# A convolution and locality-routed experts on one core: 512-row blocks by seven products, with whole sequences routed at once

## The chip, the cores and the metric

One core of one Trainium2 chip runs the kernel. The metric is device time in microseconds (us), the median of several runs. TensorE is called PE in the profile, VectorE DVE, ScalarE ACT, GpSimd POOL, and SP is the queue that issues most transfers.

## The reference

The input x has 8 sequences of 3584 tokens with 192 channels (28672 tokens in all). A causal convolution of 7 taps, whose taps are a softmax per head (8 heads of 24 channels), gives y. Then each token is routed to one of 8 experts and goes through that expert's two layers, everything in float32:

```
logits = y @ w_gate                       # [.., 8]
local  = sigmoid(y @ w_local)
e[s]   = argmax(logits[s]) if s == 0 or local[s] < 0.5 else e[s-1]
out[s] = softmax(logits[s])[e] * (relu(y[s] @ w1[e]) @ w2[e])   # w1 192x1024, w2 1024x192
```

An expert can be carried over from the token before, so routing is a scan along the sequence.

## The kernel before

**Groups.** Tokens are cut into 16 groups of 1792 (half a sequence), 14 per partition. `load_x` brings a group with a halo of 6 tokens; `conv` makes y with one ACT tap and six DVE taps for each head (L377, L387). `logits` transposes y on DVE (L570), does 96 matmul records (L580) and copies the result back; `route` finds expert, probability and slot with some 90 small DVE operations; `put` scatters 128 rows of y at a time into the DRAM array `slots`, sorted by expert (L775, POOL). Groups 0 and 1 take a faster way, `wide` and `wide_route`, before the first block.

**Blocks.** `slots` is worked off in blocks of rows of one expert. A table written by DVE (`table`) gives each block its first unit of 128 rows and its expert; SP reads an entry into a register and loads the rows (`load_rows`, L911) and the expert's weights (`load_w`, L904, 1.5 MB). A block number stands for a row count fixed when the kernel is built; only which rows and which expert is decided on the chip. There are 55 blocks of 128 rows ("singles": 35 in front, while few tokens are routed, and 20 at the end for what is left over; two more wait behind a test that reads the table) and 87 of 256 rows ("pairs"). A pair that the table marks full can be fixed ahead because so many tokens routed guarantee so many full pairs (`_sure`).

**One block.** `turn` transposes rows on PE (L359) and ACT copies them to xT (L949). D = 192 is three pieces of 64 rows, and w1 lies so that the two halves of PE's rows work on the two halves of F at once. `hidden` does h = relu(x w1) (L963 on PE, L968 on ACT), `output` does h w2 (L980), scales one half on ACT (L988), scales and adds the other on DVE (L992), and POOL sends the rows to their tokens (L996). The heart of `hidden` before is

```
for two in range(2):
    hps = [hps_p.tile([P, 2, BT], F32, name="hps") for half in range(2)]
    for d in range(KD):                    # 3 pieces of D
        for j in range(2):
            for half, rows in halves():    # L963: 24 matmuls a block, 48 records
                nc.tensor.matmul(hps[half][:, j, w], lhsT=wb[rows, f0:f0 + P], rhs=xT[rows, d, w], ...)
```

Other lines that are named below: L223 a POOL copy of y for the front's transposes, L298 a one-column POOL add of constants, L453 a transpose in `wide_route`, L550 the one-hot matrices of the first two blocks' gather, L682 the one-hot of the experts in `route`.

**The order.** Everything is written out by hand. Block i issues hidden(i), the transposes of block i+1, output(i). Between them `step(t)` issues DVE work of `conv` and `route` until the times that their `yield`s state add up to t; scatters hang behind chosen PE or ACT instructions. `ensure` loads rows up to three blocks ahead and, where a group that a block needs isn't routed or scattered yet, forces the work at once. Weights are loaded three blocks ahead into four buffers.

Of the kernel before, what the change touches and what calls it, by code (L numbers as in the profile page):

```python
# [33 lines left out]
NX = NT + HALO  # L34
# [4 lines left out]
KT = BT // P  # L39
# [4 lines left out]
EARLY = 3  # L44
SPARE = 2

# [5 lines left out]


ONE = [_sure(min(g + 1, EARLY) * PT, UT) for g in range(NPART)]
TWO = [_sure((g + 1) * PT - ONE[-1] * UT, BT) if g >= EARLY else 0 for g in range(NPART)]


HALF = 0.5
FULL = {0: ONE[0], HALF: _sure(PT + PT // 2, UT), **{g: ONE[g] for g in range(1, NPART)}}
REST = NU - ONE[-1] - 2 * TWO[-1]  # L60
# [21 lines left out]
def kernel(  # L82
# [13 lines left out]
    xs = ctx.enter_context(tc.tile_pool(name="xs", bufs=2))  # L96
    ys = ctx.enter_context(tc.tile_pool(name="ys", bufs=4))
# [3 lines left out]
    xp = ctx.enter_context(tc.tile_pool(name="xp", bufs=6))  # L101
    tp = ctx.enter_context(tc.tile_pool(name="tp", bufs=1))
    hp = ctx.enter_context(tc.tile_pool(name="hp", bufs=1))
    op = ctx.enter_context(tc.tile_pool(name="op", bufs=2))
    xps_p = ctx.enter_context(tc.tile_pool(name="xps_p", bufs=1, space=PSUM))
    hps_p = ctx.enter_context(tc.tile_pool(name="hps_p", bufs=4, space=PSUM))
    yps_p = ctx.enter_context(tc.tile_pool(name="yps_p", bufs=2, space=PSUM))
# [6 lines left out]
    def load_x(g):  # L114
        x_sb = xs.tile([P, NX, D], F32, name="x_sb")
        src = x[g // PER]
        win = bass.AP(tensor=src.tensor, offset=src.offset + g % PER * PT * D,
                      ap=[[NT * D, P], [1, NX * D]])
        nc.sync.dma_start(out=x_sb.rearrange("p t d -> p (t d)"), in_=win)
        return x_sb  # L120

    def load_b(g):

        x_sb = xs.tile([P, NX, D], F32, name="x_sb")
        xv = x_sb.rearrange("p t d -> p (t d)")[:, :NB * D].rearrange("p (b d) -> p b d", d=D)
        for b in (slice(0, NH), slice(NH, NB)):
            nc.sync.dma_start(out=xv[:, b, :], in_=xb[g, :, b, :])
        return xv
# [9 lines left out]
    with tc.tile_pool(name="scr", bufs=1) as scr:  # L138
# [4 lines left out]
        x_in = {0: load_b(0)}  # L143
        wg = cst.tile([P, 3 + DQ, Q], F32, name="wg")
        nc.sync.dma_start(out=wg, in_=wgl)
        x_in[1] = load_b(1)
# [43 lines left out]
    def z_tile():  # L190
        return yt.tile([P, 3 * NH * TB + NB * DR], F32, name="z")
# [3 lines left out]
    def wide(g, xv, y_sb, both):  # L195
# [58 lines left out]
        yr = zy[:TB, 3 * NH * TB:].rearrange("p (b d) -> p b d", d=DR)  # L254
# [17 lines left out]
        lt = sm.tile([P, NB, E + 1], F32, name="lt")[:TB]  # L272
# [9 lines left out]
    pi = cst.tile([P, 2], I32, name="pi")  # L282
    nc.gpsimd.iota(pi, pattern=[[0, 2]], base=0, channel_multiplier=1)
    ti0 = cst.tile([P, NT], I32, name="ti0")
    nc.gpsimd.iota(ti0, pattern=[[1, NT]], base=0, channel_multiplier=NT)
# [10 lines left out]
    pf = cst.tile([P, 2], F32, name="pf")  # L296
    nc.gpsimd.tensor_copy(pf, pi)
    nc.gpsimd.tensor_tensor(pf[:, 1:], pf[:, 1:], pf[:, :1], op=Alu.add)  # L298
# [32 lines left out]
    cum = cst.tile([P, 1 + E * NT], F32, name="cum")  # L331
# [5 lines left out]
    nc.sync.dma_start(out=slots[DUMMY * UT:(DUMMY + 1) * UT], in_=pad)  # L337
# [8 lines left out]
    tab = [cst.tile([P, 3], F32, name=f"tab{k}") for k in range(3)]  # L346
    ends = [cst.tile([P, 1 + E], F32, name=f"ends{k}") for k in range(3)]
    for k in range(3):
        nc.gpsimd.memset(tab[k], 0.0)
        nc.gpsimd.memset(ends[k], 0.0)  # L350
# [12 lines left out]
    def row_tile():  # L363
        return ys.tile([P, NB, DG], F32, name="y_sb")

    def conv(g, x_sb):
        y_sb = row_tile()[:, :NT, :]
        got[g] = y_sb

        def cols(h):  # L370
            return y_sb[:, :, Y0 + h * GS:Y0 + (h + 1) * GS]

        def chans(h, k):
            return x_sb[:, k:k + NT, h * GS:(h + 1) * GS]

        def first(h):
            nc.scalar.activation(cols(h), chans(h, 0), Act.Copy, scale=c[:, h, 0:1])  # L377

        first(0)
        yield 0  # L380
        for h in range(H):
            if h + 1 < H:
                first(h + 1)
            if h == H // 2 and 2 < g < NPART - 1:
                x_in[g + 1] = load_x(g + 1)
            for k in range(1, KC):
                nc.vector.scalar_tensor_tensor(cols(h), chans(h, k), c[:, h, k:k + 1],  # L387
                                               cols(h), Alu.mult, Alu.add)
                yield 0.6
# [3 lines left out]
    def wide_route(g, y_sb, lt):  # L393
# [16 lines left out]
        ex = sm.tile([P, NB, E], F32, name="ex")[:TB]  # L410
# [3 lines left out]
        eq = sm.tile([P, NB, E], F32, name="eq")[:TB]  # L414
# [13 lines left out]
        def norm():  # L428
            nc.vector.tensor_reduce(rs, ex, axis=AX.X, op=Alu.add)
            nc.vector.tensor_scalar(rs, rs, 1e-9, None, Alu.add)  # L430
            nc.vector.reciprocal(rs, rs)
# [42 lines left out]
        upto = sm.tile([P, E, 1 + NB], F32, name="upto")  # L474
# [90 lines left out]
    def logits(g, y_sb):  # L565

        z = z_tile()[:, :NT * D].rearrange("p (t d) -> p t d", d=D)
        for t in range(0, NT, TQ):
            u = min(t + TQ, NT)
            nc.vector.transpose(z[:, t:u, :], y_sb[:, t:u, Y0:Y0 + D])  # L570
            yield 0.2 * (u - t)
        yield "hop"


        lps = [hps_p.tile([P, TQ * Q], F32, name="hps") for half in range(2)]
# [658 lines left out]
```

## Time and profile before

| | us |
|---|---|
| median of 3 runs (1315.73 to 1316.56) | 1316.22 |
| the profiled execution | 1326.81 |
| its span, first to last instruction | 1325.1 |
| PE busy | 1304.4 |
| DVE busy | 778.3 |
| ACT busy | 625.2 |
| POOL busy | 480.4 |
| PE records L963 (hidden), union | 637.2 |
| PE records L980 (output), union | 641.0 |

DMA read 277.29 MB and wrote 45.77 MB, 244 GB/s over the span. The mean granted clock of TensorE was 0.998. In the profile's groups a line is: place in the code, engine, operation, output <- inputs, shapes, count | busy time, mean of one in ns | idle time before them and what ended it. In the order of time a line is: start, length, engine, place, operation, and how many were merged; [idle before <- what ended it].

### The profile page before, as it was taken

The numbers are of one execution on the slowest core, as the hardware profiler recorded it, in microseconds if no ns is written. First come the engines' busy times: TensorE is split into PE (matmuls) and PEld (weight loads), VectorE is DVE, ScalarE is ACT, GpSimd is POOL, SyncE is SP. The second block draws the span as 40 slices with busy tenths as digits, with TensorE's granted clock in tenths as the row PEclk, the third lists the DMA queues.
The fourth block names the chain that finished last, engine by engine and source line by source line (L and its number), as shares of the span: only waits on it lengthen the run. The fifth ranks groups of instructions, "written<-read, shape, count | busy, mean of one in ns | idle before, by whom it ended". The sixth has DMA issues, their size and how long they took to land. (4 is left out here: it accounts for less than half of the span.)

```text
span 1325.1 us, 41356 instructions
## 1 busy us (share of the span) xinstructions
PE 1304.4 (98%) x16682; PEld 1260.9 (95%) x16682; DVE 778.3 (59%) x2434; ACT 625.2 (47%) x1571; POOL 480.4 (36%) x520
## 2 busy tenths in 40 slices
PE   9899999999999999999999999999999999999997
PEld 7799999999999999999999999999999999999997
DVE  6888898977878787878777878785610000000000
ACT  5345555544454545444545454544444444444553
POOL 4445352534343434343434343434344212211111
PEclk9999999999999999999999999999999999999999
DMA  5789999967575757575757575756565555556893
GB/s 188 283 349 391 376 365 345 394 213 266 182 275 177 290 188 277 201 260 192 271 186 273 193 271 199 267 195 210 197 211 205 189 185 188 192 187 229 313 317 131
DMA packets 67298, 325.29 MB, mean 245 GB/s; under 512 B 12576, under 2 KB 38103, under 8 KB 47650
## 3 DMA queue, kind: packets, MB, share of 16 engines
q1 hardware_dynamic: 44784, 277.41, 58.4%
q0 software_dynamic: 22320, 45.22, 9.2%
q8 instruction: 133, 2.18, 0.7%
q14 instruction: 59, 0.48, 0.1%
q10 hardware_dynamic: 2, 0.00, 0.0%
HBM read 277.29 MB, written 45.77 MB: 244 GB/s over the span
## 5 line engine op out<-in xcount | busy, mean ns | idle before, releaser
L980 PE MATMUL yps<-wb,hT 64*128 64x192 f32 x7328 | 641.0, 325 | 5.8 <-ACT hT L968 2.8
L963 PE MATMUL hps<-xT,wb 64*128 64x256 f32 (+1 forms) x6816 | 637.2, 336 | 1.7 <-issue 1.4
L963 PEld LDWEIGHTS hps<-xT,wb 64*128 64x128 f32 x6816 | 589.1, 187 | 27.2 <-issue 4.0
L980 PEld LDWEIGHTS yps<-wb,hT 64*128 64x128 f32 x7328 | 602.8, 187 | 11.1 <-issue 4.6
L996 POOL DMA_INDIRECT out_dram<-o_sb,xg x229 | 232.3, 1014 | 605.7 <-DVE o_sb L992 533.9
L968 ACT ACTIVATE hT<-hps 128x512 f32<-128x512 f32 (+1 forms) x568 | 261.9, 512 | 361.4 <-PE hps L963 246.5
L387 DVE SCALAR_TENSOR_TENSOR y_sb<-x_sb,c,y_sb 128x336 f32<-128x336 f32 x672 | 376.5, 570 | 18.9 <-issue 0.8
L992 DVE SCALAR_TENSOR_TENSOR o_sb<-yps,xg,o_sb 128x192 f32<-128x192 f32 x229 | 87.5, 414 | 467.8 <-ACT o_sb L988 461.4
L775 POOL DMA_INDIRECT slots<-y_sb,posi x228 | 231.2, 1014 | 209.3 <-ACT xT L949 114.8
L988 ACT ACTIVATE o_sb<-yps,xg 128x192 f32<-128x192 f32 x229 | 86.9, 418 | 289.8 <-PE yps L980 287.4
L949 ACT COPY xT<-xps 64x256 f32<-64x256 f32 (+4 forms) x568 | 210.8, 371 | 11.7 <-issue 1.7
L377 ACT ACTIVATE y_sb<-x_sb,c 128x336 f32<-128x336 f32 x112 | 63.7, 581 | 0.0
L359 PEld LDWEIGHTS xps<-ident,xg 64*128 64x128 f32 (+1 forms) x916 | 57.0, 124 | 5.2
L359 PE MATMUL xps<-ident,xg 64*128 64x64 f32 (+1 forms) x916 | 60.0, 217 | 0.0
L570 DVE STREAM_TRANSPOSE z<-y_sb 128x768 f32<-128x768 f32 (+1 forms) x56 | 45.4, 853 | 0.4
L596 DVE COPY lt<-lq 32x36 f32<-32x36 f32 x224 | 40.8, 182 | 3.5
L580 PE MATMUL hps<-z,wg 64*32 64x128 f32 x1344 | 24.2, 272 | 1.2 <-issue 1.2
L580 PEld LDWEIGHTS hps<-z,wg 64*32 64x32 f32 x1344 | 19.2, 105 | 4.1 <-issue 2.9
L556 PE MATMUL yps<-y_sb,hot 112*128 112x194 f32 x64 | 12.6, 353 | 1.4 <-DVE hot L550 1.1
L556 PEld LDWEIGHTS yps<-y_sb,hot 112*128 112x128 f32 x64 | 11.3, 202 | 2.1 <-DVE hot L550 1.6
L672 DVE COPY bk<-so_far 1x32 f32<-1x32 f32 x56 | 12.3, 220 | 0.7
L588 DVE STREAM_TRANSPOSE lq<-ls 128x256 f32<-128x256 f32 x14 | 6.2, 441 | 10.9 <-ACT ls L585 10.9
(236 smaller groups left out, 358.0 us busy)
## 6 DMA issues: line engine op xcount, KB each, us to landing
wb<-in_w_dram SPq DMA_DIRECT2D x138, 1536.0 KB
x_sb<-in_x_dram SPq DMA_DIRECT2D x14, 1920.0 KB
xg<-slots SPq DMA_DIRECT2D x87, 195.0 KB
wb<-in_w_dram SPq DMA_DIRECT2D x12, 512.0 KB
xg<-slots SPq DMA_DIRECT2D x53, 97.5 KB
out_dram<-o_sb,xg POOLq DMA_INDIRECT x229
slots<-y_sb,posi POOLq DMA_INDIRECT x228
x_sb<-in_xb_dram SPq DMA_DIRECT2D x4, 768.0 KB
```

What stands on the lines that cost most here:

```text
L359: nc.tensor.transpose(to, src[rows], identity=ident[rows, rows])
L377: nc.scalar.activation(cols(h), chans(h, 0), Act.Copy, scale=c[:, h, 0:1])
L387: nc.vector.scalar_tensor_tensor(cols(h), chans(h, k), c[:, h, k:k + 1], cols(h), Alu.mult, Alu.add)
L570: nc.vector.transpose(z[:, t:u, :], y_sb[:, t:u, Y0:Y0 + D])
L775: ins = nc.gpsimd.indirect_dma_start(out=slots[:, :], in_=rows, in_offset=None, out_offset=bass.IndirectOffsetOnAxis(ap=to, axis=0)).ins
L949: copied = nc.scalar.copy(a, b)
L963: nc.tensor.matmul(hps[half][:, j, w], lhsT=wb[rows, f0:f0 + P], rhs=xT[rows, d, w], start=(d == 0 and j == 0), stop=(d == KD - 1), skip_g ...
L968: relu = nc.scalar.activation(hT[:, m:m + 2, w], hps[half][:, :, w], Act.Relu)
L980: nc.tensor.matmul(yps[half][:, k * D:(k + 1) * D], lhsT=hT[rows, m, k * P:(k + 1) * P], rhs=wb[rows, WA + m * D:WA + (m + 1) * D], start= ...
L988: nc.scalar.activation(o_sb[:, k, :], y[k][0], Act.Copy, scale=xg[:, k, 0:1])
L992: nc.vector.scalar_tensor_tensor(o_sb[:, k, :], y[k][1], xg[:, k, 0:1], o_sb[:, k, :], Alu.mult, Alu.add)
L996: sent = nc.gpsimd.indirect_dma_start(out=out, in_=o_sb[:, k, :], in_offset=None, out_offset=bass.IndirectOffsetOnAxis(ap=xg.bitcast(I32)[ ...
```

## The change

- **Groups.** Groups 0 to 3 stay half sequences; the other twelve become six whole sequences of 28 tokens per partition (`GROUPS`), so `route` runs 8 times and not 14. `logits` does a whole sequence in two parts, each in two visits that are placed inside `output` and the next `step`, in whichever PSUM pool is free there.
- **x by heads.** x is laid out by head on the host. A unit of load and conv is one head of one group (64 units). Six are loaded in front on SP's queue, the others by `taps` on ACT's queue, at most two a block; `taps` also issues first taps ahead of `conv`.
- **Blocks.** 51 singles, 20 pairs, 31 blocks of 512 rows, 14 singles. How many blocks of a kind a group allows is no longer what is guaranteed (`_sure`) but that less a constant (`_likely`; LEFT1 640, LEFT2 1408, LEFT 2900, LEFT3 1152); a block that doesn't fill points to a dummy unit, and 28 spare singles wait behind two tests.
- **Seven products.** A block of 512 rows takes `seven` and not `hidden`. Two of the three pieces of D, two halves of the rows and two halves of the columns make a 2x2x2 product by seven products of combined operands; the third piece adds four plain ones. `combine_w` makes the weights' combinations on POOL one block ahead, `combine_x` those of the rows on DVE.
- **PSUM.** From the first block on there are four pools of one tile of two banks: `xps_p`, `wps_p`, `yps_p`, `zps_p`. `output` runs in parts of at most 256 rows; `turn` is cut into `turn_out` (PE) and `turn_in` (ACT).
- **Order.** `step` carries what it overshot to the next one. Budgets: single 2.3, 1.3, 1.4 (before 2.1, 1.2, 1.3), pair 4.7, 1.3, 3.6 (before 4.2, 1.2, 3.0), 512 rows 2.4, 4.4, 1.6, 1.4. Scatters are spread: about 2 a single, 4 a pair, 6 a block of 512. In front, `step` 0.6 stands where 1.8 and 2.4 stood.

```diff
-EARLY = 3
+EARLY = 4
-ONE = [_sure(min(g + 1, EARLY) * PT, UT) for g in range(NPART)]
-TWO = [_sure((g + 1) * PT - ONE[-1] * UT, BT) if g >= EARLY else 0 for g in range(NPART)]
+def _likely(tokens, size, left):
+    return max(0, (tokens - left) // size)
+GROUPS = [*range(EARLY)] + [*range(EARLY + 1, NPART, 2)]
+ONE = {g: _sure((g + 1) * PT, UT) if g + 1 < EARLY else _likely(EARLY * PT, UT, LEFT1) for g in GROUPS}
+TWO = {g: min(PAIRED, _likely((g + 1) * PT - ONE[LAST] * UT, BT, LEFT2)) if g >= EARLY else 0 for g in GROUPS}
+FOUR = {g: _likely((g + 1) * PT - PAST, QT, LEFT if g < LAST else LEFT3) if g + 1 >= FIRST else 0 for g in GROUPS}
...
+    def combine_w(wb):
+        nc.gpsimd.tensor_tensor(wt[:, 1, :], b22, b12, op=Alu.subtract)
+        yield
+        nc.gpsimd.tensor_tensor(b12, b12, b11, op=Alu.subtract)
+        yield
+        nc.gpsimd.tensor_tensor(wt[:, 0, :], b22, b12, op=Alu.subtract)
+        yield
+        nc.gpsimd.tensor_tensor(wt[:, 2, :], b21, wt[:, 0, :], op=Alu.subtract)
+        yield wt
+    def combine_x(xT):
+        nc.vector.tensor_tensor(xc[:, 0, :], xT[:, 0, one], xT[:, 0, two], op=Alu.subtract)
+        nc.vector.tensor_tensor(xT[:, 0, two], xT[:, 0, two], xT[:, 1, two], op=Alu.add)
+        nc.vector.tensor_tensor(xc[:, 1, :], xT[:, 0, two], xT[:, 0, one], op=Alu.subtract)
+        nc.vector.tensor_tensor(xc[:, 2, :], xT[:, 1, one], xc[:, 1, :], op=Alu.subtract)
+        nc.vector.tensor_tensor(xc[:, 3, :], xT[:, 2, one], xT[:, 2, two], op=Alu.subtract)
+    def seven(wb, wt, xT, xc, turn_next, weights_next):
+        def times(to, a, b, first=False):        # one product: 4 matmuls of 64x256
+            for j in range(2):
+                for half, rows in halves():
+                    ins = nc.tensor.matmul(to[:, half, j, :], lhsT=b[rows, j * P:(j + 1) * P],
+                                           rhs=a[rows, :], start=(first and j == 0), stop=True, ...)
+            return ins
+        times(xb, a11, b11, True)
+        nc.scalar.copy(h11, xb)
+        times(yb, s1, t1, True)
+        times(yb, a23, b32)
+        nc.scalar.copy(h22, yb)
+        times(xb, s2, t2)
+        nc.scalar.copy(h12, xb)
+        put(times(wbk, a12, b21, True))
+        times(wbk, a13, b31)
+        step(SIDE[0], None, 1)
+        nc.vector.tensor_tensor(h11, wbk, h11, op=Alu.add)
+        nc.scalar.activation(h11, h11, Act.Relu)
+        put(times(xb, s3, t3))
+        nc.vector.tensor_tensor(h22, xb, h22, op=Alu.add)
+        nc.scalar.activation(h22, h22, Act.Relu)
+        times(yb, s4, b22)
+        put(times(yb, s5, b32))
+        at = turn_next()
+        times(xb, a22, t4)
+        wt = weights_next()
+        next(wt)
+        put(times(xb, a23, b31))
+        next(wt)
+        nc.vector.tensor_tensor(h12, yb, h12, op=Alu.add)
+        nc.scalar.activation(h12, h12, Act.Relu)
+        nc.scalar.activation(h21, xb, Act.Relu)
...
-            for k in range(1, KC):
-                nc.vector.scalar_tensor_tensor(cols(h), chans(h, k), c[:, h, k:k + 1], cols(h), Alu.mult, Alu.add)
-                yield 0.6
+        for k in range(1, KC):
+            nc.vector.scalar_tensor_tensor(cols, x_in[u][:, k:k + n, :], c[:, h, k:k + 1], cols, Alu.mult, Alu.add)
+            yield 0.6 if n == NT else 1.0
...
     def step(time, bank=None, early=0):
...
+        time += st["over"]
         while time > 0:
...
+        st["over"] = min(time, 0)
...
-        "x": xp,
+        "x": xp.reshape(B, S + HALO, XQ, DH).transpose(0, 2, 1, 3),
```

In `seven`, a11, a12, a13 are the first 256 rows' three pieces of D and s1, a22, a23 the second's (s1 is the sum of its first two pieces, made in place), b11 to b32 the pieces of w1 by the two column halves (t1 made in place of b12); s2 to s5 come from `combine_x`, t2 to t4 from `combine_w`. xb, wbk and yb are tiles of `xps_p`, `wps_p` and `yps_p`.

## The prediction

> **What bounds the kernel now.** The page's first two parts come first: which engine is full, and when.
>
> ```profile
> PE 1304.4 (98%) x16682; PEld 1260.9 (95%) x16682; DVE 778.3 (59%) x2434; ACT 625.2 (47%) x1571; POOL 480.4 (36%) x520
> ...
> PE   9899999999999999999999999999999999999997
> ...
> DVE  6888898977878787878777878785610000000000
> ...
> DMA  5789999967575757575757575756565555556893
> ```
>
> TensorE (PE) is busy in every slice; VectorE (DVE) is the only other engine near full, and only until the routing ends two thirds through; DMA is full in the first quarter and at the end. So TensorE's work is the time, plus what it waits. The table of stretches says where it waits:
>
> ```profile
> core 0: us, PE busy (x) PEld busy (x) DVE busy (x) ACT busy (x) POOL busy (x), PEclk, DMA share, GB/s
> ...
> 46.00:76.00 30.00, 25.92 (x373) 24.73 (x373) 27.48 (x85) 13.69 (x42) 13.78 (x14) 0.99 0.80 298
> 76.00:260.00 184.00, 180.74 (x2961) 175.76 (x2958) 160.40 (x483) 100.71 (x314) 82.70 (x82) 1.00 0.96 368
> ...
> 940.00:1208.00 268.00, 268.00 (x3018) 251.53 (x3016) 33.81 (x138) 111.77 (x252) 72.16 (x74) 1.00 0.56 193
> ```
>
> The first 35 blocks, of 128 rows, end near 258 us; there DMA is at 0.96. The pairs (256 rows) have no idle TensorE. The order of time of TensorE gives the price of a block, from one hidden matmul group (L963) to the next, of a pair and of a single:
>
> ```profile
> 1177.03 5.34 PE L963 MATMUL hps<-xT,wb 64*128 64x256 f32 x48
> 1182.21 0.39 PE L359 MATMUL xps<-ident,xg 64*128 64x64 f32 x8
> 1182.44 5.42 PE L980 MATMUL yps<-wb,hT 64*128 64x192 f32 x64
> 1187.69 5.34 PE L963 MATMUL hps<-xT,wb 64*128 64x256 f32 x48
> ...
> 1225.77 2.84 PE L963 MATMUL hps<-xT,wb 64*128 64x128 f32 x48
> 1228.44 0.28 PE L359 MATMUL xps<-ident,xg 64*128 64x64 f32 x4
> 1228.56 2.82 PE L980 MATMUL yps<-wb,hT 64*128 64x192 f32 x32
> 1231.21 2.84 PE L963 MATMUL hps<-xT,wb 64*128 64x128 f32 x48
> ```
>
> A pair takes 1187.69 - 1177.03 = 10.66 us: hidden 5.18, transposes 0.23, output 5.25. A single takes 5.44. The 24 matmuls of `hidden` are 48 records, so one product of `seven` (4 matmuls, 8 records of the same 64x256 shape) is 5.18/6 = 0.863 us. Prices for the other engines come from the groups by shape:
>
> ```profile
> L968 ACT ACTIVATE hT<-hps 128x512 f32<-128x512 f32 x348 | 189.5, 595 | 288.9 <-PE hps L963 204.2 <-PE xps L359 78.9 <-issue 5.8
> ...
> L968 ACT ACTIVATE hT<-hps 128x256 f32<-128x256 f32 x220 | 72.5, 381 | 72.5 <-PE hps L963 42.3 <-PE xps L359 14.4 <-ACT o_sb L988 7.8
> ...
> L550 DVE TENSOR_TENSOR hot<-rel,wb 112x512 f32<-112x512 f32 x8 | 5.1, 691 | 0.0
> ...
> L223 POOL COPY z<-y_sb 112x512 f32<-112x512 f32 x4 | 2.6, 655 | 10.6 <-DVE y_sb L216 5.9 <-DVE at L479 4.7
> ```
>
> **The change part by part, 1: the blocks.** The constants give 51 singles, 20 pairs, 31 blocks of 512 rows ("fours"), no late pairs and 14 last singles, against 55 singles and 87 pairs: 229 units of 128 rows both times. I routed the reference's own inputs by expert and group: all 51, 20 and 31 fill, and exactly 14 part-filled units remain, so no block is a dummy and the 28 spare ones stay behind their `If`. A four issues 11 products where two pairs issue 12: a 2x2x2 scheme of seven products on two of the three 64-row pieces of D (eight before), four plain products on the third. 11 x 0.863 = 9.50, four units of transposes 0.46, output 2 x 5.25: 20.46 us, against 21.32. Sum: singles +10 x 5.44 = +54.4, pairs -67 x 10.66 = -714.2, fours +31 x 20.46 = +634.3: **-25.5 us**, all of it on TensorE, which sets the end.
>
> **2: what `seven` asks of the others.** Every sum of products now goes through three PSUM tiles, one buffer each, so TensorE waits for ScalarE (ACT) and VectorE inside the block. Prices: ACT goes from 381 to 595 ns for 256 more elements, so 1024 take about 1.02 us; DVE 691 ns at 512 and 275 at 112 (L682) give 1.04 ns an element, about 1.23 us. From the block's first matmul: last block's two output scales end at 0.93 (as now); copy of h11 1.06 to 2.08, needed free at 2.59; copy of h22 2.79 to 3.81; copy of h12 to 4.83, needed at 5.18. The three adds on DVE start when the fifth and sixth products end (5.18 + 0.2) and end at 6.6, 7.9 and 9.1; the tiles they free are wanted at 7.8, 8.2 and 10.0. No wait, by margins of 0.3 to 1.2 us. The side work in front of the adds (`step`, 2.4) ends by about 4.2, the one-block-ahead `combine_x` (five ops of 256, 0.42 each) runs under the second half of the output. DVE sum: 3.7 + 2.1 + four scaled adds 1.7 + steps 9.8 = 17.3 of 20.5. POOL: four sends and six scatters of 1.0 (L996, L775), four `combine_w` ops. The trace has no POOL add of 256; its 112x512 copy is 655 ns, its 1-element add 195 (L298), so 0.2 to 0.7 each: 11 to 13 of 20.5. Queued behind a late add on DVE are the other two, the scaled adds and the taps; behind a late copy on ACT the relus and `turn_in`, which the next block needs 6 us later; behind a scatter that waits for its product on POOL is a `combine_w`, wanted 8 us or more later, in the next block (t1, t3, t2), or 20 later (t4). Bounds per four: nothing, or 0.3 (the smallest margin, used up by late copies); below nothing is excluded, since the products themselves are counted. I take 0.05: **+1.5**, range 0 to +9.
>
> The Trainium skill, "SBUF — State Buffer", "Who interferes with whom", speaks against this part: a DVE op with two SBUF inputs and a POOL op that reads SBUF lock each other out for a whole instruction. No row here shows a POOL add beside such a DVE op; by the rule each four would lose some of four POOL ops' time on DVE, and as DVE has 3 us of slack a block the sum would stay.
>
> **3: the early singles.** From 73.45 (block 4) to 257.8 there are 31 blocks and three logits (2.38, 2.41, 2.09): (184.3 - 6.9)/31 = 5.72 a block, 0.28 over the clean one. Bytes explain it: weights 1.57 MB, rows read, scatters and output 0.1 each, x 4 x 1.97/31 = 0.25: 2.12 MB, at 368 GB/s 5.77 us. After: by head, 20 or 34 tokens a partition, 8.7 MB of x over blocks 4 to 50 = 0.19, so 2.06 MB or 5.59 us, 0.15 over clean; 47 x 0.15 = 7.1 against 8.7: **-1.5**. Bounds: the old loss on 16 more blocks, +4.5; none left, -8.7. The x loads move from SP's to ACT's queue; a DMA issue on SP takes 0.33, so some 0.3 us of ACT per block, which is half idle there. A load that finds its slot still read by DVE would hold ACT's next scales and relus; it is issued only once that head's taps stand in DVE's order a block earlier, so I cost it at nothing, 0.1 a single if not (it is inside the +4.5). The skill's "DMA: Bandwidth & Descriptors", "Measured", advises transfers of 1 MiB and more and gives 78% of peak at that size; x now comes in 245 and 418 KB pieces, for which this trace has no row; by it these bytes would cost a quarter more, an estimate of +5.
>
> **4: logits and side work.** Fourteen passes of 96 matmuls stay; one costs 1.6 in the pairs, 2.1 to 2.4 in the singles. The conv's adds fall from 672 of 336 elements (570 ns) to 96 of those and 288 of 672 (some 0.92 by the same slope), 376 to 320 us, and 14 routings become 8: worth nothing while DVE is covered. Walking the new order by the costs its `yield`s state (5.0 a single, 9.6 a pair, 9.8 a four) puts six passes among the singles (four now), +1.4; each is split in two visits, 0 to 0.2 each; hidden where the switch falls in a wait. **+2**, range -3 to +4. By the same walk groups 2, 3, 5, 7, 9, 11, 13, 15 are routed at blocks 12, 23, 39, 53, 60, 68, 77, 84, all ahead of the first block that needs them (21, 35, 51, 62, 71, 77, 84, 91); only at block 49 are five scatters forced together, so that block 51's rows may come late: 0 to +2.5, **+1**. DVE in an early single: 5.0 x 0.97 (570 ns and gap for a stated 0.6) + 0.41 = 5.3 of 5.44: tight, as now.
>
> **5: the front.** The same 16 scatters, side work 0.6 where 4.2 stood, x loads of 1.47 MB instead of 1.97; in return new PSUM and SBUF pools wait for the old ones' readers. TensorE idles 2.0 us before L453 now. **-1**, range -3 to +3.
>
> Sum: -25.5 + 1.5 - 1.5 + 2 + 1 - 1 = -23.5. The profiled execution took 1326.81 us, span 1325.1, 10.6 above the median of 1316.22; I expect a span near 1301.6 and, the same difference taken off the median, **1293 us**.
>
> **The rivals.** (a) *The chain inside a four shows* (chance 0.08, slower): three 1024-element adds between 5.4 and 10.0. If such an add on PSUM and SBUF takes over 1.5 us, output waits for the third; the kernel is slower once a four loses more than 0.76 us (23.5/31), at adds of 1.8 us. At 2.0: 1.4 lost x 31 = +43, 1336 us. Against it: 691 ns at 512 and 958 at 768 (L570). For it: 0.41 for 192 from PSUM (L992) is steeper. (b) *It shows a little* (0.22): copies 0.15 late and a lock now and then, 0.4 a four: 1305 us; it also covers early singles that lose 0.5 each. (c) *The early loss goes* (0.12): with x smoother, -8 more: 1285. (d) *No change* (0.05): 0.7 a four, 1315. (e) *A table falls short and spare blocks run* (0.01): 26 x 5.44 and more, above 1430; the counts exclude it. The forecast itself: 0.52, 1287 to 1300.
>
> **How the numbers follow.** The range takes in (b) and (c) and leaves out (a), (e) and most of (d): 1281 to 1311. A change within 0.2% (2.6 us) can't be told from none. Faster is the forecast, (b) and (c): 0.86; same (d) 0.05; slower (a) and (e): 0.09.
>
> **What would show it.** Fours of 20.4 to 20.6 us from block to block on TensorE, 88 records of 64x256 each; 1024-element ACT copies near 1.0 and DVE adds near 1.25; singles early near 5.6; six logits before the pairs. I am wrong if TensorE idles before a product or an output in the fours for DVE h11, h22, h12 or ACT, or if early singles go above 5.8.

## The result: slower, where 1293 us was forecast

The changed kernel takes 1324.68 us (median of 7 runs, 1321.21 to 1328.40) against 1316.04 of the kernel before beside it (1315.19 to 1317.71): a ratio of 1.0066, 95% interval 1.0051 to 1.0082. The profiled execution took 1324.68 us, with a span of 1322.7.

The first and second part of the page after, the lines that answer to those shown of before:

```profile
PE 1281.7 (97%) x16674; PEld 1229.1 (93%) x16674; DVE 825.1 (62%) x1891; ACT 690.5 (52%) x1402; POOL 618.9 (47%) x650
...
PE   9989999999899999999999999999997999999997
...
PEclk9999999999899999999999999999998999999999
DMA  5899989989967677665443524244325333233483
```

TensorE did lose work: 1304.4 busy us fell to 1281.7, by 22.7 (busy time counts matmuls at half clock too, and the page of before most likely comes from a slower chip; against the 1296.5 of b1, below, it is 14.8). Two slices (11th and 31st) show a lower clock, and the 31st a hole. So the saving was made, and time was lost around it. The groups of waits of TensorE name the holes (engine and line, what it waited for, us in total, times, longest):

```profile
PE ps L400 <- DMA xg<-slots: 13.5, 3, 8.7
PE ps L1172 <- ACT h L1080: 5.4, 4, 3.2
PE ps L400 <- DVE h L1142: 3.3, 2, 1.7
PE ps L1076 <- issue: 1.9, 2, 1.0
PE ps L1172 <- DVE o_sb L1188: 1.6, 2, 1.0
PE ps L1127 <- DVE h L1145: 1.6, 3, 0.5
```

**The base.** Kernels that were run together ran on one chip, and the chips differ: the kernel before took 1315 to 1316 us on two of them and 1329 to 1333 on three. In all 16 runs below the profiled execution lies within 5 us of its kernel's median, so the 10.6 us between the profile of before (1326.81) and its median (1316.22) are most likely a chip's and not a profile's. On a chip where before takes 1315.34, I profiled it again (b1, below). With that, the two kernels can be laid side by side. "Lost" is the time from a block's first hidden matmul to the next block's, less a clean block: 5.444 for a single, 10.665 for a pair, 20.42 for a four.

| us | before (b1) | after | difference |
|---|---|---|---|
| first block starts | 43.9 | 42.6 | -1.3 |
| clean blocks | 1227.3 | 1200.2 | -27.1 |
| lost in the early singles (35, 51) | 16.4 | 37.4 | +21.0 |
| lost in the pairs (87, 20) | 19.1 | 8.9 | -10.2 |
| lost in the 31 fours | - | 24.9 | +24.9 |
| last matmul to the end | 6.7 | 8.7 | +2.0 |
| span | 1313.5 | 1322.7 | +9.2 |

Logits account for 26.5 of before's loss (7.6 in the singles, 19.0 in the pairs) and for 30.3 of after's (13.2, 8.4 and 8.7).

**A clean four** in the order of time of TensorE, after (start, us, count of records, idle time before in brackets):

```profile
880.58 2.76 PE L1127 MATMUL ps<-xT,wb 64*128 64x256 f32 x24
883.17 1.03 PE L1127 MATMUL ps<-xc,wt 64*128 64x256 f32 x8
...
890.60 10.57 PE L1172 MATMUL ps<-wb,h 64*128 64x192 f32 x128
901.00 1.25 PE L1127 MATMUL ps<-xT,wb 64*128 64x256 f32 x10
```

901.00 - 880.58 = 20.42 us, with no idle time: 20.46 was forecast.

**Block 90**, the largest hole, all engines in order of time:

```profile
988.73 1.91 PE L1127 MATMUL ps<-xc,wb 64*128 64x256 f32 x16
...
992.00 0.96 POOL L871 DMA_INDIRECT slots<-pad,toi  x1 [0.30 <-issue]
993.25 0.96 POOL L871 DMA_INDIRECT slots<-pad,toi  x1 [0.30 <-issue]
996.13 2.14 SPq L1016 DMA_DIRECT2D xg<-slots  x3
...
999.33 1.12 PE L400 MATMUL ps<-ident,xg 64*128 64x64 f32 x16 [8.68 <-DMA xg<-slots]
```

TensorE wants to transpose the rows of block 91 at 990.6. `ensure` had to force six scatters on POOL first (986.95 to 994.21); only when the last had landed did SP issue the rows (996.13), and they came at 999.3. The six are `fill`'s pad scatters, which only the last singles read. Block 50, in the order of time of TensorE, has the same hole behind the five scatters forced at block 49:

```profile
352.40 0.69 PE L400 MATMUL ps<-ident,xg 64*128 64x64 f32 x8 [4.21 <-DMA xg<-slots]
352.88 4.92 PE L1172 MATMUL ps<-wb,h 64*128 64x192 f32 x32
357.65 2.54 PE L1076 MATMUL ps<-xT,wb 64*128 64x256 f32 x22
```

The second line is a second loss: an output of 32 records takes 2.7 elsewhere and 4.92 here. The table of stretches says why; the column behind POOL is the granted clock:

```profile
80.67:84.08 3.41, 3.41 (x22) 3.41 (x24) 3.11 (x6) 1.78 (x7) 2.09 (x2) 0.50 0.79 253
350.33:357.16 6.83, 4.76 (x36) 4.76 (x38) 0.60 (x2) 1.68 (x4) 0.00 (x0) 0.50 0.85 280
995.45:1002.28 6.83, 2.96 (x26) 2.75 (x28) 0.00 (x0) 0.00 (x0) 0.00 (x0) 0.50 0.70 207
```

Behind each long wait the clock stands at half for one or two stretches of 3.41 us. So block 50 loses 6.96 us by a wait of 4.21, and block 90 loses 10.3 by one of 8.68. The Trainium skill states this in "TensorE: Matmul & The Clock Gate", Part 1, on the clock gate: a free-running window of 3413 ns, half the clock after an idle one. The trace agrees in the length, and the three starts lie whole windows apart (79 and 268 of them from the first). It does not agree in the idle window: in the 3.41 us that end at 350.33 TensorE is busy for 1.28. The prediction had no price for this.

**Block 5** is the x load on ACT's queue, all engines in order of time:

```profile
73.47 2.38 DVE L463 SCALAR_TENSOR_TENSOR y_sb<-x_sb,c,y_sb 128x336 f32<-128x336 f32 x4
...
74.20 0.42 ACT L1182 ACTIVATE o_sb<-ps,xg 128x192 f32<-128x192 f32 x1 [0.95 <-PE ps L1172]
...
75.77 0.41 DVE L1188 SCALAR_TENSOR_TENSOR o_sb<-ps,xg,o_sb 128x192 f32<-128x192 f32 x1
...
79.36 0.33 ACTq L156 DMA_DIRECT2D x_sb<-in_x_dram  x1
79.75 0.58 ACT L425 ACTIVATE y_sb<-x_sb,c 128x336 f32<-128x336 f32 x1 [5.13 <-DMA wb<-in_w_dram]
80.23 1.18 ACT L1080 ACTIVATE h<-ps 128x256 f32<-128x256 f32 x4
...
80.64 4.55 PE L1172 MATMUL ps<-wb,h 64*128 64x192 f32 x32 [3.19 <-ACT h L1080]
```

ACT stands from 74.62 to 79.36 at the issue of an x load; its relus, behind it in order, come at 80.23; TensorE waits 3.19 and then runs its output at half clock. The load did not wait for its slot: DVE had ended its adds at 75.85 and then only did a scaled add, to 76.18. The waits of ACT name what let it go, and SP's queue shows a weight load issued some 11 us before:

```profile
ACT y_sb L425 <- DMA wb<-in_w_dram: 5.1, 1, 5.1
```

```profile
68.33 1.32 SPq L1009 DMA_DIRECT2D wb<-in_w_dram  x2
```

In the trace the x load waits on the semaphore on which the weight load of 68.33 counts its landing, and that landing ended at 79.29. The three other holds of ACT by an x load of over 0.8 us (2.25 in block 27, 0.89 and 0.96) end in the same way, with a transfer that SP issued 5 to 11 us before. So do the longest ones in a0, a1, f1 and h2 (2.2 to 3.7 us, at block 7), with a weight load.

**Block 72** is one of two fours (with 79) whose adds are late:

```profile
605.95 0.88 ACT L425 ACTIVATE y_sb<-x_sb,c 128x672 f32<-128x672 f32 x1
606.86 2.83 DVE L463 SCALAR_TENSOR_TENSOR y_sb<-x_sb,c,y_sb 128x672 f32<-128x672 f32 x3 [3.86 <-ACT y_sb L425]
609.60 1.22 DVE L1142 TENSOR_TENSOR h<-ps,h 128x1024 f32<-128x1024 f32 x1
...
610.88 0.69 PE L400 MATMUL ps<-ident,xg 64*128 64x64 f32 x16 [1.65 <-DVE h L1142]
```

There a new unit of the convolution starts in `step`: its tap (L425) queues on ACT behind the copy of h12, DVE waits 3.86 us for the tap, does its side work, and the add of h11 ends 1.65 us after TensorE needs its tile.

### The profile page after: what moved, and what is told of

It is laid out like the page before. It is cut to its first block, busy times and chain, and to the rows that moved or that the text cites. A ratio compares the mean times of both kernels' runs of the same rounds, so it can differ in the third digit from the quotient of the medians.

```text
span 1322.7 us, 40921 instructions
## 1 busy us (share of the span) xinstructions
PE 1281.7 (97%) x16674; PEld 1229.1 (93%) x16674; DVE 825.1 (62%) x1891; ACT 690.5 (52%) x1402; POOL 618.9 (47%) x650
## 5 line engine op out<-in xcount | busy, mean ns | idle before, releaser
L1172 PE MATMUL ps<-wb,h 64*128 64x192 f32 x7328 | 629.7, 326 | 7.0 <-ACT h L1080 5.4
L1172 PEld LDWEIGHTS ps<-wb,h 64*128 64x128 f32 x7328 | 600.8, 188 | 12.2 <-ACT h L1080 6.7
L463 DVE SCALAR_TENSOR_TENSOR y_sb<-x_sb,c,y_sb 128x672 f32<-128x672 f32 (+1 forms) x384 | 321.6, 846 | 49.8 <-ACT y_sb L425 41.0
L1076 PE MATMUL ps<-xT,wb 64*128 64x128 f32 (+1 forms) x4080 | 295.4, 297 | 3.5 <-issue 1.9
L1076 PEld LDWEIGHTS ps<-xT,wb 64*128 64x128 f32 x4080 | 275.1, 188 | 17.6 <-issue 4.5
L1188 DVE SCALAR_TENSOR_TENSOR o_sb<-ps,xg,o_sb 128x192 f32<-128x192 f32 x229 | 87.6, 412 | 319.6 <-ACT o_sb L1182 317.4
L1182 ACT ACTIVATE o_sb<-ps,xg 128x192 f32<-128x192 f32 x229 | 87.3, 418 | 312.8 <-PE ps L1172 302.7
L1080 ACT ACTIVATE h<-ps 128x256 f32<-128x256 f32 (+1 forms) x340 | 128.3, 431 | 142.3 <-PE ps L1076 139.7
L1054 ACT COPY xT<-ps 128x128 f32<-128x128 f32 (+2 forms) x464 | 194.2, 418 | 11.7 <-PE ps L400 5.1
L1127 PE MATMUL ps<-xT,wb 64*128 64x256 f32 x1488 | 177.3, 376 | 0.0
L1127 PEld LDWEIGHTS ps<-xT,wb 64*128 64x128 f32 x1488 | 150.4, 187 | 8.6
L425 ACT ACTIVATE y_sb<-x_sb,c 128x672 f32<-128x672 f32 (+1 forms) x64 | 50.8, 796 | 17.6 <-DMA wb<-in_w_dram 5.1
```

Source lines behind the costliest of these rows:

```text
L425: nc.scalar.activation(got[g][:, :, Y0 + h * GS:Y0 + (h + 1) * GS], x_in[u][:, :n, :], Act.Copy, scale=c[:, h, 0:1])
L463: nc.vector.scalar_tensor_tensor(cols, x_in[u][:, k:k + n, :], c[:, h, k:k + 1], cols, Alu.mult, Alu.add)
L1054: copied = nc.scalar.copy(a, b)
L1076: nc.tensor.matmul(hps[:, half, j, :], lhsT=wb[rows, f0:f0 + P], rhs=xT[rows, d, :], start=(d == 0 and j == 0), stop=(d == KD - 1), skip_g ...
L1080: relu = nc.scalar.activation(hT[two][:, half], hps[:, half], Act.Relu)
L1127: ins = nc.tensor.matmul(to[:, half, j, :], lhsT=b[rows, j * P:(j + 1) * P], rhs=a[rows, :], start=(first and j == 0), stop=True, skip_gro ...
```

## The experiments

Four sets of four kernels, in the order in which they ran. Before took 1331.83 us in the first set, 1332.78 in the second, 1315.34 in the third, 1329.11 in the fourth.

**c0: the kernel before again.** No edit.

> The kernel before, unchanged, beside the others, for a second profile of it. If the profiled execution shown of before was typical, this one has a span near 1325 us again with 14 us lost by the early singles (beyond their clean 5.44 us and the logits), and the 10.6 us between it and the median are the price of being profiled. If that execution was an unlucky one, this span is near 1315 and the early singles lose some 4 to 8 us only; then the sum of the prediction took its -23.5 from too high a base, by up to 10 us.

1331.86 us, ratio 1.0006 (0.9996 to 1.0016), span 1328.2; it loses 27.3 us in the early singles and 19.9 in the pairs. On this chip the kernel before is 1.2% slower than on the chip of the result.

**e1: more scatters per block.**

```diff
-            if shares and (n == 2 or two or st["block"] % 2 and len(to_put) > NT):
+            if shares:
...
-            if n == KT and part == 0 and two != k:
+            if n == KT and two != k:
...
-                if k:
+                if k and part == 0:
```

> The changed kernel with scatters issued sooner: three a single and eight a 512-row block while any are waiting. Theory: two waits for rows (4.2 us in front of block 51, 8.7 in front of block 91, with some 2 us of slow TensorE after each) come from scatters that the order left until a load needed them; without them 1324 falls by 12 to 17 us, to 1307 to 1312, and no TensorE idle time is put down to DMA of rows. Rival: the transfers themselves are late (a full DMA); then the waits stay and the time falls by less than 4 us.

1372.22 us, ratio 1.0317 (1.0285 to 1.0349). Both waits for rows are gone, and others have come; the waits of TensorE:

```profile
PE ps L1127 <- ACT h L1138: 9.8, 5, 2.3
PE ps L1076 <- issue: 8.3, 19, 1.1
PE ps L1172 <- issue: 6.5, 10, 1.1
PE ps L1172 <- ACT h L1080: 4.4, 8, 1.5
```

The early singles lose 60.7 us (47.4 and 51.7 in e2 and e3, on the same chip) and the fours 34.9. So more scatters in every block cost more than the two waits that they remove, and the rows have to be in time without them. Why ACT's copies come late is not shown; that POOL, at 47% of the span in after, has no room is a guess.

**e2: x loads on SP's queue.**

```diff
-        (queue or nc.scalar).dma_start(out=x_sb.rearrange("p t d -> p (t d)"), in_=win)
+        (queue or nc.sync).dma_start(out=x_sb.rearrange("p t d -> p (t d)"), in_=win)
```

> The changed kernel with all x loads issued on SP's queue, as before the change. Theory: on ACT's queue an x load that can't be issued yet holds the relus behind it (block 5 lost 5.2 us, blocks 27 and 46 some 3 together); on SP's queue these go, the time falls by 4 to 9 us. Rival: what holds ACT is the DMA itself, full of weights; then block 5 waits all the same, or the weights come later, and the time changes by less than 3 us or rises.

1346.47 us, ratio 1.0107 (1.0083 to 1.0131). Block 90 still waits 8.6 us, block 5 is clean. The changed kernel itself was not in this set, so the price was left to f2 and h2.

**e3: a twelfth product in each four** (it is added to a sum where it doesn't belong, so the output is not the reference's).

```diff
         put(times(xb, a23, b31))
+        times(xb, a23, b31)
```

> The changed kernel with a twelfth product in each 512-row block (the last one issued twice, so its output is not the reference's): as many products as two pairs take. Theory: these blocks are bound by TensorE alone, so 31 x 0.863 = +26.8 us. Rival: the block has slack hidden in waits for ACT and DVE; then it rises by less than 20 us.

1378.86 us, ratio 1.0354 (1.0337 to 1.0372). Two fours in the order of time of TensorE:

```profile
900.64 2.75 PE L1127 MATMUL ps<-xT,wb 64*128 64x256 f32 x24
...
921.92 2.75 PE L1127 MATMUL ps<-xT,wb 64*128 64x256 f32 x24
```

921.92 - 900.64 = 21.28, 0.86 above 20.42: a product costs its own time and nothing hides it. The saving of one product a four is real.

**a0: the changed kernel again.** No edit.

> The changed kernel once more, beside the kernel before and three versions, all on one chip. Theory 1 (what the chips differ by was taken for a loss of the old kernel): the ratio to before stays within 1.004 to 1.016, whatever the chip; the stages lose the same as in the first profile of it, 37 us over clean blocks in the early singles, 9 in the pairs, 25 in the fours, within 8 each. Rival (the first profile was unlucky, with two long waits that come and go): the waits ahead of blocks 51 and 91 are not there again and the ratio is below 1.0.

1355.28 us, ratio 1.0158 (1.0135 to 1.0180). Block 90 waits 8.60 us again, so that wait is no accident. But the early singles lose 54.0 us, not 37, and the pairs 15.3: my theory was wrong in that the stages would lose the same on every chip. Its span is 34.0 us longer than in the first profile: 16.7 are lost in the early singles, of which the changed kernel has 16 more than before, 6.4 in the pairs, 4.6 in the fours, 4.6 ahead of the first block and 1.5 at the end.

**b0: the kernel before, beside it.** No edit.

> The kernel before, profiled beside the changed one. Theory 1: on a chip where it takes about 1316 us its early singles lose some 13 us over 35 clean blocks instead of the 23 of the profile that the prediction used, and its pairs 20, nearly all of it logits; on a chip where it takes 1326 or more, 23 to 28. Rival: the early loss is 23 everywhere, and the base of the sum was right.

1330.51 us, ratio 0.9985 (0.9974 to 0.9997), span 1330.1. It loses 28.8 us in the early singles, 20.2 in the pairs. Nothing was changed here, and the interval still leaves out 1: a difference of 2 us between two medians is not to be read.

**f1: rows in time.** The pads belong to the last singles alone, and the group of blocks 51 to 61 goes out at three scatters a single.

```diff
-            to_put.append((g, pad, toi[:, e:e + 1]))
+            to_put.append((g + 1, pad, toi[:, e:e + 1]))
...
+    def need(i):
+        return blocks[i][3] + (blocks[i][0] == 4)
...
-            if shares and (n == 2 or two or st["block"] % 2 and len(to_put) > NT):
+            if shares and (n == 2 or two or (st["block"] % 2 and len(to_put) > NT or st["routed"] == 5)):
```

> Three scatters in every early single once the group of blocks 51 to 61 is routed, so that all 28 are out before block 49 (none forced), and the eight pad scatters marked as belonging to the last singles alone, so that block 91 waits for its group's own scatters only. Number of scatters unchanged. Theory 1 (these two forced bursts and the slow clock after each idle stretch cost 10.3 and 6.9 us): 12 to 18 us below the changed kernel, a ratio to before of 0.993 to 1.0 on a quick chip, and blocks 50 and 90 lose under 1 us each. Rival (the rows wait for DMA bandwidth, not for the scatters): the two waits stay and the time moves by under 4 us. Rival 2 (three scatters a single make the early blocks later by as much): block 50's loss goes, but blocks 40 to 48 lose 3 us or more in all.

1342.40 us, ratio 1.0063 (1.0047 to 1.0080): 12.9 below a0. Theory 1 holds in the fours: they lose 17.9 instead of 29.5, block 90 under 0.5 instead of 11.6. At block 50 the loss goes (6.2 to under 0.5), but rival 2 is right as well: blocks 44 to 47 now lose 15.1 us where they lost 6.6, a logits pass being among them both times. The gain is the pads'; what block 50 no longer loses is lost ahead of it.

**f2: rows in time and x on SP's queue.** The edits of f1 and e2.

> As the version with rows in time, and the x loads of the side work issued on SP's queue again instead of ACT's. Theory 1 (an x load on ACT's queue holds the relus behind it while it waits for its slot; 5.2 us at block 5 and 2 at block 27): 5 to 8 us below the version with rows in time. Rival (on SP the same wait holds the weights and rows behind it): within 3 us of it, or slower.

1338.88 us, ratio 1.0045 (1.0028 to 1.0062): 3.5 below f1, between theory 1 and its rival. This trace shows best what a wait costs; TensorE in order of time, and the table of stretches:

```profile
331.74 1.57 PE L1175 MATMUL ps<-wb,h 64*128 64x192 f32 x16 [2.13 <-ACT h L1083]
```

```profile
333.19:343.43 10.24, 9.30 (x70) 8.47 (x68) 4.93 (x7) 2.97 (x10) 6.05 (x6) 0.50 1.01 381
```

One wait of 2.13 us is followed by three windows at half clock, in which TensorE is busy for 9.30 of 10.24 us: block 46 loses 6.19 us with only 0.94 of idle time. Why those relus were late stays open: the profile puts the 3.05 us that ACT stood ahead of them down to "remote", to nothing on this core.

**g1: three mended.** f2 with two and three scatters in turn until block 50, the tap of a new unit right behind the copy of h11, and without the 26 last spare blocks.

```diff
-            if shares and (n == 2 or two or (st["block"] % 2 and len(to_put) > NT or st["routed"] == 5)):
+            if shares and (n == 2 or two or st["block"] % 2 and (len(to_put) > NT or st["routed"] == 5)):
...
         nc.scalar.copy(h11, xb)
+        start_route()
+        start_conv()
...
-        if spare[SPARE:]:
-            with left(spare[SPARE:]):
-                also(spare[SPARE:])
```

> The version with rows in time and x on SP's queue, with three edits in stages apart: (1) two and three scatters in turn in the singles before block 51 instead of three in each, (2) in a four the next unit's first tap is put on ACT right behind the copy of h11 instead of behind the copy of h12, (3) the 26 last spare blocks are left out of the program (no row of these inputs is in them). Theory 1: (1) three scatters of 1.0 to 1.5 us and a send with 0.3 us between them fill POOL's 5.44 us, so that sends, the slots of o_sb, ACT's scales and TensorE come late: blocks 40 to 50 lose 4 to 8 us less; (2) blocks 71, 72 and 79 lose 4 to 6 us less; (3) the time from TensorE's last matmul to the end of the span falls from 10.8 to 7 us. Together 10 to 17 us below the version with rows in time and x on SP, at or just under before. Rival for (1): the loss of those blocks comes from full DMA and goes on, within 2 us; for (2): the add is late through DVE's own queue, and block 72 still waits 1.7 us; for (3): the end is the last send's landing, and stays.

1299.01 us, ratio 0.9886 (0.9863 to 0.9909): 16.3 us below before. Against the first profile of the changed kernel, on a chip where before takes the same: the early singles lose 24.2 instead of 37.4, the fours 12.0 instead of 24.9, the end takes 6.7 instead of 8.7. The waits of TensorE that are left (its rows at blocks 6 and 50, and block 79):

```profile
PE ps L400 <- DMA xg<-slots: 3.9, 2, 2.3
PE ps L400 <- DVE h L1147: 1.7, 1, 1.7
PE ps L1177 <- ACT xT L1057: 1.5, 1, 1.5
PE ps L1079 <- issue: 1.5, 2, 1.3
```

Of (1), blocks 40 to 50 lose 7.0 us, 4.3 of them in blocks with logits; f2 ran on a slower chip, so the two can't be set against each other, and that POOL was full there is not shown. Of (2), blocks 71, 72 and 79 lose 3.6 instead of 6.2: the early tap mended 72 but not 79. Of (3), the end is as expected.

**g2: half the weights for blocks 4 to 50** (their output matmuls read the first half twice, so those outputs are not the reference's).

```diff
+        upto = WA if AHEAD < i < 51 else WA + WB
...
+        w0 = 0 if AHEAD < st["block"] < 51 else WA
```

> The changed kernel with only the first half of the weights loaded for blocks 4 to 50, whose output matmuls read that half twice (so the outputs of these blocks are not the reference's). The matmuls are the same; 0.79 MB of DMA a single are gone, over a third of what a single moves. Theory 1 (the early singles lose to DMA at its limit, as the prediction's byte count says): the 51 singles lose 15 to 25 us less than in the changed kernel on the same kind of chip, that is 12 to 22 us on a quick chip and 29 to 39 on a slow one. Rival (they lose to the order on ACT, DVE and POOL: relus behind a tap or an x load, sends behind scatters): under 6 us less, and the waits for ACT h stay.

1314.01 us, ratio 0.9993 (0.9983 to 1.0003). The early singles lose 24.1 us, 13.3 less than in the first profile of the changed kernel, a little short of theory 1 and far from the rival, with the DMA share from 150 to 250 us at 0.74 instead of 0.97. Most of what went is the wait of ACT at block 5 (5.2), the one at block 27 (1.9) and the `issue` waits at blocks 19 and 35 (2.6); the waits for rows at blocks 50 (3.6) and 90 (8.5) stayed. So full DMA makes the x load's wait long, as its end at the landing of a weight load (block 5, above) has it. Both theories have a share: what the wait holds is ACT's order.

**g3: one add of six.** For every unit behind the first six one add of the convolution is left, so logits and outputs are not the reference's.

```diff
+            if k == 1:
                 nc.vector.scalar_tensor_tensor(cols, x_in[u][:, k:k + n, :],
                                                c[:, h, k:k + 1], cols, Alu.mult, Alu.add)
```

> The changed kernel with one of the six adds of the convolution kept for every unit behind the first six (the logits and so the outputs are not the reference's; routing, scatters and rows stay as busy, though the counts by expert change). Takes some 265 us of VectorE's work away, most of it before block 90. Theory 1 (VectorE at 5.3 of 5.44 us a single, as the prediction works it out, is what makes scales and sends late): the early singles lose 10 us or more less. Rival (DVE is covered): within 4 us of the changed kernel in the early singles; the two adds that were late in blocks 72 and 79 stay, since they wait for the tap.

1496.59 us, ratio 1.1381 (1.1362 to 1.1400). As a whole this says nothing of the adds: other logits give other counts by expert, and the spare blocks ran (181 us behind the last block). By stage it does: the early singles lose 31.9 instead of 37.4, between the two theories, with block 5 still at 5.26. The wait of 1.65 us for the first add in blocks 72 and 79 is gone, against my expectation: the adds that follow the tap are in its length too.

**b1: the kernel before, a third time.** No edit.

> The kernel before, profiled on this chip. Theory 1: where it takes about 1316 us its early singles lose 11 to 16 us over clean blocks; where it takes 1326 or more, 23 to 29. Rival: 23 everywhere.

1315.67 us, ratio 1.0006 (0.9997 to 1.0016). It loses 16.4 us in the early singles: 7.6 in blocks 0 to 2, 7.6 with the four logits, and 1.2 in all other blocks together. The rival (23 everywhere) is wrong.

**a1: the changed kernel a third time.** No edit.

> The changed kernel as the base of this call. On a chip where before takes about 1316 us: 1322 to 1329, ratio 1.005 to 1.009, early singles 34 to 41 us over clean; on a slow one 1350 to 1358, ratio 1.014 to 1.018, 50 to 57 over clean. Rival: other numbers, so that something else than the chip decides.

1347.53 us, ratio 1.0135 (1.0116 to 1.0155), on a chip between the two kinds; the early singles lose 49.4, the fours 27.2.

**h1: nothing left out.** g1 with its 26 spare blocks back.

> The version with three mended, with its 26 last spare blocks back: rows in time (pads waited for by the last singles alone, two and three scatters in turn to the end of block 50), x on SP's queue, the next unit's tap behind the copy of h11, all rows of any input covered. Theory 1 (the spare blocks cost 2 to 4 us at the end and nothing elsewhere): ratio to before 0.989 to 0.992 on a quick chip, 0.994 to 1.001 on a slow one; 8.5 to 11 us from TensorE's last matmul to the end of the span. Rival: the end stays at 6.7, and the version with three mended owed nothing to leaving them out.

1327.86 us, ratio 0.9992 (0.9980 to 1.0005), beside 1347.53 of the changed kernel. From TensorE's last matmul to the end of the span 9.3 us, where g1 had 6.7: the spare blocks cost 2.6 at the end though none runs (the two ran on different chips, but before takes 6.8 there in all four of its profiles). The kernel is 19.7 us better than the changed one here, and no better than before: on this chip its early singles lose 44.2.

**h2: x on ACT's queue.** h1 with e2's edit undone.

> As the version with nothing left out, x loads back on ACT's queue. Theory 1 (a load that finds its slot still read holds ACT's relus): 6 to 12 us slower than the version with nothing left out, the loss at block 5 (5 us with the slow clock) and at a few blocks behind it. Rival (a stage's wait moves from ACT to SP, where rows and weights stand behind the load): within 3 us.

1334.77 us, ratio 1.0042 (1.0022 to 1.0062): 6.9 slower than h1 (the two profiled executions differ by 3.7). The size is theory 1's; its mechanism is not shown. The loss is spread over blocks 6, 7, 45 and 50 and not at block 5, and the one hold of ACT of over 2 us by an x load (2.19, block 7) ends with a weight load's landing.

**h4: logits in one visit.**

```diff
-            st["bank"], st["due"], st["half"] = bank, False, True
-            route_op()
+            st["bank"], st["due"] = bank, False
+            route_op()
+            route_op()
```

> As the version with nothing left out, both halves of a logits pass issued in one visit instead of two. Theory 1 (each of the two switches between output and logits costs 0.2 us on TensorE): a pass costs 1.7 to 1.8 us instead of 2.1 in the pairs and fours, 14 passes give 4 to 6 us. Rival (the pass costs the same, since it is the 96 matmuls that do): under 1.5 us.

1325.73 us, ratio 0.9979 (0.9962 to 0.9995): 2.1 below h1, with intervals that overlap. In an undisturbed four the pass costs 1.72 instead of 2.14, so the split has its price, about what theory 1 says. The total didn't follow: the early singles lose more again (46.8 against 44.2), with `issue` waits inside the passes, and of the 3.8 us that the fours lose less, 2.6 are block 79, with a shorter wait and no half clock behind it.

## Why the prediction was wrong, step by step

**The blocks (-25.5): right.** Fours of 20.42, singles of 5.44, pairs of 10.66: -27.1 us, and e3 shows that each product stands on the path.

**What `seven` asks of the others (+1.5): mis-sized.** The copies (1.01 us), the adds (1.22) and `combine_x` (0.42) took what was forecast, and 28 of the 31 fours lose nothing but logits and, in block 90, the wait for rows. Blocks 71, 72 and 79 lose 6.2 together. The statement that failed is that the side work ahead of the adds "ends by about 4.2": in 72 and 79, at the start of a unit, it waits for a tap on ACT that stands behind three 1024-element copies, and in 72 it ends 8.4 us into the block. Block 71, the first four, loses 1.0 without such a tap: there `combine_x` itself runs to 580.6, 0.8 into the block, and DVE's side work ends 6.8 into it. The skill's lock between DVE and POOL, which spoke against this part, can be seen in the groups by shape and in block 72: a POOL add of 256 takes 0.73 us at the median and 1.12 beside the convolution's adds, three of which then take 3.16 us instead of 2.83. As forecast, that is too small to show in the sum.

**The early singles (-1.5): wrong in base and in size.** Away from blocks 0 to 2, 50 and the logits, after loses 13.1 us more than clean blocks where before loses 1.2. The 0.28 a block that I wanted to improve on came from a profile of a slower chip: b1 shows 0.04. The step that failed is the price of the x loads on ACT's queue: "A load that finds its slot still read by DVE would hold ACT's next scales and relus [...] I cost it at nothing". The slot was free in time, as it said, but a load can stand for another reason, and at block 5 one held ACT for 4.7 us until a weight load had landed; the block lost 5.2. The medians give 3.5 (f1 against f2) to 6.9 us (h2 against h1) for the queue. The rest goes with full DMA over more blocks: with half the weights (g2) 13.3 us of the loss are gone. How much of it is due to x's smaller pieces no run tested alone.

**Logits and side work (+2): +3.8**, inside its range; of this the split is a part (1.72 against 2.14 a pass).

**The forced scatters (+1): the step with the largest miss.** They cost 17.3 us: 6.96 at block 50 and 10.3 at block 90. I saw the first and priced its wait at 2.5 at most, without the half clock behind it. The second was missing from my walk: it ended with the routing of group 15 "all ahead of the first block that needs them (21, 35, 51, 62, 71, 77, 84, 91)" at block 84, and left out the tables and `fill`'s eight pads, which carry the group's number and so hold block 91's rows. f1 shows it: the pads alone, moved behind, give the fours 11.6 us back (f1 against a0, on one chip).

**The front (-1): -4.9** (1.3 in the start of block 0, 3.6 in blocks 0 to 2), beyond its range of -3 to +3 and no merit of the walk: on the chip of a0 and b0 the same two places cost 3.1 more than before. **The end: not in the sum**, +2.0, from 28 spare blocks where 2 stood (h1 against g1: 2.6).

The sum of these is -27.1 + 6.2 + 11.9 + 3.8 + 17.3 - 4.9 + 2.0 = 9.2 us, as much as the spans differ by. None of the rivals was it: (a) and (b), a chain inside each four, are excluded by 20.42, and the loss came from waits that each happen in a few blocks and from the early singles, which (b) had at 0.5 each and which lose 0.71 each from block 4 to 50. Both signs that the prediction named for being wrong came: TensorE idles for DVE's h in blocks 71, 72 and 79, and these early singles take 6.15 us each (5.77 without block 50 and those with logits).

## What to carry to other kernels

A stall of TensorE is priced by the wait and by the half clock that can follow it: waits of over 2 us cost from none to three windows of 3.41 us at half speed. When work is spread over queues, walk the queue to the very last item, padding and tables too, and ask which read waits for each; a marker that is too coarse (pads in the group of the rows) cost 10.3 us here, of the 27.1 that the rewrite saved. An issue on a compute engine's queue holds that engine for whatever the transfer waits for, not only for its buffer. Before a loss in the profile is taken as something to win, see whether the profile and the median agree.

## What the runs showed of the hardware

The clock fell behind windows of 3.41 us that were idle in part only: 2.13 us ahead of the fall at 350.33 in after, 1.96 ahead of the one at 333.19 in f2. It did not fall behind every such wait: in g1 block 50 has one of 2.25 us and block 79 2.21 us of idle time, and they lose 2.70 and 2.60. What decides stays open. The `issue` waits of TensorE, which the profile gives to nothing, go together with the queue that it calls "instruction". In f2, block 35, order of time of TensorE, and the DMA queues from 263 to 266.6 us:

```profile
266.40 1.83 PE L1079 MATMUL ps<-xT,wb 64*128 64x128 f32 x29 [2.88 <-issue]
```

```profile
q8 instruction: 1, 0.02, 1.7%
```

That packet of 16 KB landed 1.4 us before the matmuls went on; the `issue` wait of the same block has such a packet 1.2 to 1.5 us before its end in after, a0 and f1 as well. With half the weights' bytes (g2) this wait was gone. That TensorE waited for its instructions behind full DMA is the reading that fits; no run tested it alone. Of the 16.6 us by which b0's span is longer than b1's, 12.4 are lost in the early singles, where DMA is full. Why stays open, and so does whether it is the chip or the time at which a set ran.
